# First group of a chunked attention with a maxout product behind it: another order for the first microseconds, with two tiles' scores taken at once

## The chip, the cores and the metric

The kernel runs on one core of one Trainium2 chip. The metric is device time in microseconds (us); a version's time is the median of its runs.

## The reference

```python
# q, k, v: (8, 8, 576, 64) -> batch, heads, sequence, head size; chunks of 64 rows
scores = scale * q_c @ k_c.T            # within each chunk alone, 64 x 64
attn = exp(scores - max) ; attn /= (sum(attn) + 1e-9)
x = (attn @ v_c), heads side by side    # 4608 tokens x 512
h = max(x @ w1, x @ w2, x @ w3)         # 512 -> 768, three products, largest kept
out = h @ w_out                         # 768 -> 512
```

Everything is float32.

## The kernel before

**Tiles and groups.** The 4608 tokens are 36 tiles of 128. Eight of them make two groups of four (columns of a 512 wide moving operand); the other 28 run in four later units. The change touches the first group alone: tiles 0 to 3, with tiles 4 to 7 begun among them, and the loading of all weights, which happens only here.

**Precision.** A float32 product is made of three products of reduced floats: each operand is split into a high part and the rest, and `three` (L186 to L189) multiplies low by high, high by low and high by high. So both the weights (`wh`, `wl`) and the attention's result (`xh`, `xl`) need a high and a low part before a product can start.

**Order.** Nothing is reordered by a scheduler: the engines (PE, DVE, ACT, POOL and the DMA queue SP) take their instructions in the order in which the program calls them, and wait for each other by semaphores. For the first group that order is written by hand in the table `FIRST` (L45), a list of names that `first_group` (L801) calls one after the other. The names are:

- for attention tile *t*: `q`t, `v`t loads; `S`t scores on PE (L237, 16 products of 64x64); `mx`t maximum (DVE, L242); `sub`t subtract it (DVE, L247); `exp`t (ACT, L251); `sum`t (DVE, L195); `eps`t add 1e-9 (DVE, L198); `rec`t reciprocal (DVE, L201); `nrm`t normalise (L204; on POOL with a `p` behind the name, else on DVE); `T`t transposes (PE, L260) into the bank `tp`; `at`t copy of `tp` (ACT, L265); `V`t product with the values (PE, L296); `xh`t and `xl`t high and low part of the result (ACT L303, DVE L307).
- for weight piece *j w* (128 of 768 columns, matrix 1 to 3): `W` load of 512 KB (L154); `A` exponent part (ACT, L163); `B` scaled low words (ACT, L168); `C` shift (DVE, L172); `X` add (POOL with a `p`, else DVE, L176); `H` high part `wh` (ACT, L179); `Y` low part `wl` (POOL with a `p`, else DVE, L182).
- `h`jw with `a` or `b`: products of piece *jw* with columns 0 to 255 (tiles 0 and 1) or 256 to 511 (tiles 2 and 3), 12 matmuls each; with `f` all 512 columns. `F` is the running maximum of the three results, `hh` and `hl` its split.
- `i`n: n idle products of zeros (L795), which only keep PE at work.

The scores of tiles 0 to 3 go into one pair of PSUM banks (`ps_s`), two tiles in turn; `V` writes another pair (`ps_x`), of which tiles 0 and 2 use one half and tiles 1 and 3 the other. The framework follows dependencies by whole PSUM tiles where it can't tell halves apart.

Of the kernel before, what the change touches and what calls it, by code (L numbers as in the profile page):

```python
# [42 lines left out]


FIRST = """  # L45
q0 i13 W01 A01 S0 i5 mx0 q1 sub0 W00 C01 exp0 sum0 S1 mx1 sub1 B01 q2 A00 exp1 W12 eps0 v0 q3 i8 rec0 B00 X01p S2 sum1
H01 mx2 eps1 nrm0p T0 at0 rec1 v1 sub2 nrm1p V0 T1 exp2 C00 S3 X00p xh0 q4 W02 at1 B12 sum2 H00 eps2 V1 rec2 mx3 xh1
nrm2p sub3 T2 S4 xl0 exp3 xl1 sum3 at2 Y00p v2 B02 W10 eps3 rec3 v3 nrm3 A02 W20 h00a V2 A12 C02 W31 T3 Y01p A10 xh2
X02 H02 at3 C10 W11 C12 X12p F00a h01a Y02 V3 xl2 B10 xh3 B31 q5 X10p xl3 A20 W21 A11 h02a F01a H12 F02a B11 C11 W61
W52 Z B20 B21 W40 H10 mx4 sub4 hh0a exp4 W22 C20 X20 W32 Y12 X11 Y10 A31 H11 W30 h01b hl0a h00b C31 h02b A21 H20 X31  # L50
S5 F00b C21 Y11 h12f F01b A40 q6 v4 H31 sum4 W41 B40 X21p h10f F02b H21 Y31 Y20 B30 hh0b eps4 hl0b Y21 C40 mx5 B61
X40p h11f h20f B32 F10f rec4 A22 sub5 W42 A32 C32 S6 A30 X32p h21f B22 W64 F11f F12f W51 C22 B52 H40 hh1f nrm4 hl1f
# [11 lines left out]
def chunk_attn_maxout_kernel(  # L64
# [147 lines left out]
    def bank_of(name):  # L212
        if name not in banks_of:
            banks_of[name] = ps[name].tile([P, 2, 2, 4, 64], F32, name=name[-1])
        return banks_of[name]

    def plain_steps(t, x_of, col):


        st = {}  # L220
# [9 lines left out]

        def scores():
            r = st["r"]
            st["s"] = s = bank_of("ps_s")[:, :, t % 2 if t < 4 or "pair" in st else 0]
            for g in range(4):
                for h, c in quarters:
                    a, b = halves_of[c], halves_of[h]
                    nc.tensor.matmul(out=s[b, c, g, :], lhsT=r[a, 0, 2 * g + h, :], rhs=r[a, 1, 2 * g + h, :],  # L237
                                     start=True, stop=True)
# [70 lines left out]
        def pair(both):  # L309
            st["pair"] = both  # L310

        return dict(q=load_qk, v=load_v, pair=pair, S=scores, mx=maximum, sub=less, exp=exp, sum=total,
                    eps=lambda: st["guard"](), rec=lambda: st["invert"](), nrm=lambda *eng: st["norm"](*eng),
                    T=transpose, at=transposed, bt=blocks, bw=to_scratch, br=from_scratch, V=values, xh=high, xl=low)
# [442 lines left out]
    def hold(name, make):  # L757
        if name not in held:
            held[name] = make()
        return held[name]  # L760
# [90 lines left out]
    def next_load(u, k):  # L851
# [5 lines left out]
        T3=lambda: hold("T3", lambda: late["hold"].tile([P, 2, 3, 256], F32R, name="T3")),  # L857
        s=lambda: hold("s", lambda: late["hold"].tile([P, 5, HALF], F32, name="kept")),
# [163 lines left out]
```

## Time and profile before

| what | value |
|---|---|
| median of 3 runs | 610.44 us (610.24 to 610.49) |
| the profiled execution, its own time | 610.66 us |
| its span on the core | 608.9 us |
| PE busy | 599.4 us (98%) |
| DVE, ACT, POOL busy | 422.8, 289.9, 187.2 us |
| PE on the chain of work that ended last | 92% |

A line of the timeline has the start (us from the span's start), the duration in us, the engine, the source line, the operation, what it writes and reads, and how many; in brackets, where the engine sat idle, for how long and what released it. A line of the windows has the stretch, its length, and the busy time of each engine in it, then the granted clock of PE, the share of the DMA engines and GB/s.

### The profile page before, as it was taken

How to read it: one execution, taken by the hardware profiler on the slowest of the kernel's cores; microseconds unless marked ns; L12 is line 12 of the kernel's file. 1: busy time of each engine (PE TensorE's matmuls, PEld its weight loads, DVE VectorE, ACT ScalarE, POOL GpSimd, SP SyncE). 2: the span in 40 equal slices, each digit the busy share in tenths (PEclk: the TensorE clock that was granted, in tenths of full speed). 3: DMA queues.
4: the chain of work that ended last, by engine and by line, in shares of the span. 5: the costliest groups of instructions: out<-in, count | busy, mean ns of one | idle time of the engine just before them, and what ended most of it. 6: DMA issues, size and time to landing. Idle time of an engine off the chain costs nothing.

```text
span 608.9 us, 12710 instructions
## 1 busy us (share of the span) xinstructions
PE 599.4 (98%) x5045; PEld 520.7 (86%) x5046; DVE 422.8 (69%) x700; ACT 289.9 (48%) x522; POOL 187.2 (31%) x168
## 2 busy tenths in 40 slices
PE   7899999999999999999999999999999999999997
PEld 3788878888899999997888888888888888999997
DVE  4898965768887986894674769936474598244373
ACT  4897734443554554555243344643333355333353
POOL 2522477777232424100250612002424000131300
PEclk9999999999999999999999999999999999999999
DMA  8987667756868998747887894568767444677532
GB/s 336 362 316 269 258 191 266 276 207 238 300 244 300 360 347 289 275 137 252 293 274 242 290 347 162 161 231 285 244 200 262 154 156 123 224 261 259 188 130 79
DMA packets 59484, 148.95 MB, mean 245 GB/s; under 512 B 5665, under 2 KB 24609, under 8 KB 59425
## 3 DMA queue, kind: packets, MB, share of 16 engines
q1 hardware_dynamic: 59424, 148.13, 69.5%
q8 instruction: 40, 0.66, 0.4%
q14 instruction: 20, 0.16, 0.1%
HBM read 116.92 MB, written 31.20 MB: 243 GB/s over the span
## 4 chain that ended last, share of the span: by engine, by line
PE 92%; DVE 5%; ACT 1%; issue 1%; DVEq 0%; ACTq 0%
PE pm L187 28%; PE pm L189 28%; PE pm L188 28%; PE s L237 3%; PE pm L296 3%; PE tp L260 1%; PE pm L795 1%; DVE H L594 1%; DVE stage L519 1%; DVE e L247 0%; DVE sm L195 0%; DVE xl L307 0%; PE s L296 0%; DVE mx L242 0%; DVE X L528 0%
## 5 line engine op out<-in xcount | busy, mean ns | idle before, releaser
L187 PE MATMUL pm<-X,ring 128*128 128x512 f32 (+1 forms) x504 | 184.4, 366 | 0.6 <-ACT kept L626 0.6
L189 PE MATMUL pm<-X,ring 128*128 128x512 f32 (+1 forms) x504 | 182.5, 362 | 0.3 <-issue 0.3
L188 PE MATMUL pm<-X,ring 128*128 128x512 f32 (+1 forms) x504 | 182.4, 362 | 0.0
L626 ACT COPY kept<-pm 128x384 f32<-128x384 f32 (+1 forms) x144 | 76.8, 534 | 155.0 <-PE pm L189 154.9
L187 PEld LDWEIGHTS pm<-X,ring 128*128 128x128 f32 x504 | 94.6, 188 | 11.6 <-ACT kept L626 1.2
L189 PEld LDWEIGHTS pm<-X,ring 128*128 128x128 f32 x504 | 94.6, 188 | 10.4 <-issue 0.6
L188 PEld LDWEIGHTS pm<-X,ring 128*128 128x128 f32 x504 | 94.7, 188 | 9.6
L632 POOL TENSOR_TENSOR kept<-kept 128x384 f32<-128x384 f32 (+1 forms) x24 | 28.6, 1193 | 128.8 <-ACT kept L626 128.8
L629 DVE TENSOR_TENSOR pm<-pm,kept 128x384 f32<-128x384 f32 (+1 forms) x48 | 30.2, 628 | 51.7 <-PE pm L189 51.7
L187 PE MATMUL pm<-xh,wl 128*128 128x512 f32 (+1 forms) x156 | 60.0, 385 | 0.0
L188 PE MATMUL pm<-xl,wh 128*128 128x512 f32 (+1 forms) x156 | 58.4, 374 | 0.3 <-DVE xl L307 0.3
L189 PE MATMUL pm<-xh,wh 128*128 128x512 f32 (+1 forms) x156 | 58.3, 374 | 0.0
L594 DVE TENSOR_TENSOR H<-most,H 128x384 fp32r<-128x384 f32 (+1 forms) x72 | 48.8, 689 | 11.5 <-ACT H L591 11.3
L635 DVE TENSOR_TENSOR most<-pm,most 128x384 f32<-128x384 f32 (+1 forms) x72 | 44.5, 618 | 10.6 <-PE pm L189 9.4
L204 POOL TENSOR_TENSOR e<-e,sm 128x512 f32<-128x512 f32 x27 | 31.5, 1168 | 63.4 <-DVE sm L201 26.5
L632 POOL TENSOR_TENSOR most<-kept 128x384 f32<-128x384 f32 (+1 forms) x12 | 13.8, 1148 | 115.0 <-ACT kept L626 115.0
L242 DVE TENSOR_REDUCE mx<-s 128x8 f32<-128x512 f32 x36 | 24.6, 684 | 33.9 <-PE s L237 33.9
L591 ACT CAST H<-most 128x384 fp32r<-128x384 f32 (+1 forms) x72 | 40.7, 569 | 10.6 <-PE pm L189 9.0
L528 DVE TENSOR_TENSOR X<-stage,X 128x768 fp32r<-128x768 f32 (+1 forms) x28 | 35.0, 1255 | 13.2 <-ACT X L524 13.0
L524 ACT CAST X<-stage 128x768 fp32r<-128x768 f32 (+1 forms) x28 | 26.2, 944 | 29.4 <-DVE stage L519 23.3
L251 ACT ACTIVATE e<-e 128x512 f32<-128x512 f32 x36 | 22.8, 632 | 28.2 <-DVE e L247 28.2
L188 PE MATMUL pm<-H,woh 128*128 128x384 f32 (+1 forms) x96 | 34.8, 363 | 0.1
(119 smaller groups left out, 1060.7 us busy)
## 6 DMA issues: line engine op xcount, KB each, us to landing
ring<-w SPq DMA_DIRECT2D x72, 768.0 KB, 6.1
buf<-in_qk SPq DMA_DIRECT2D x36, 512.0 KB, 5.8
buf<-in_vb SPq DMA_DIRECT2D x36, 256.0 KB, 6.4
ring<-w SPq DMA_DIRECT2D x36, 256.0 KB, 4.1
w<-s SPq DMA_DIRECT2D x9, 768.0 KB, 3.8
out_x<-ao SPq DMA_DIRECT2D x24, 256.0 KB, 2.8
ring<-wo SPq DMA_DIRECT2D x8, 768.0 KB, 4.9
stage<-in_w SPq DMA_DIRECT2D x7, 512.0 KB, 5.1
```

The source lines that it names most:

```text
L187: nc.tensor.matmul(out=o, lhsT=al, rhs=bh, start=first, stop=False, skip_group_check=shared)
L188: nc.tensor.matmul(out=o, lhsT=ah, rhs=bl, start=False, stop=False, skip_group_check=shared)
L189: nc.tensor.matmul(out=o, lhsT=ah, rhs=bh, start=False, stop=last, skip_group_check=shared)
L204: eng.tensor_tensor(out=e, in0=e, in1=sm.unsqueeze(2).broadcast_to([P, 8, 64]), op=ALU.mult)
L524: nc.scalar.copy(out=X[i][:, 0], in_=source[i]())
L528: return lambda: eng.tensor_tensor(out=X[i][:, 1], in0=source[i](), in1=X[i][:, 0].bitcast(F32), op=minus)
L591: nc.scalar.copy(out=H[i, jp][:, 0, :half], in_=hidden_block(i, jp))
L594: nc.vector.tensor_tensor(out=H[i, jp][:, 1, :half], in0=hidden_block(i, jp), in1=H[i, jp][:, 0, :half].bitcast(F32), op=minus)
L626: return lambda: nc.scalar.copy(out=to, in_=o)
L629: return lambda: nc.vector.tensor_tensor(out=o if w else M(jp, q), in0=o, in1=kept(k), op=plus)
L632: nc.gpsimd.tensor_tensor(out=kept(3) if w else M(jp, A22), in0=kept(3), in1=kept(p7), op=plus)
L635: return lambda: nc.vector.tensor_tensor(out=M(jp, q), in0=of, in1=M(jp, q), op=most)
```

## The change

The table gets another order for its first four lines; from `B10 B31 q5` on it is the same. The scores of tiles 0 and 1 follow each other on PE, tile 1's written into the pair of banks that `V` uses later. Eleven idle products stand ahead of them instead of thirteen; the later idle products are 6, 3, 4, 2 and 3 (before: 5 and 8). Piece 01's products come ahead of piece 00's. Tile 0 is normalised on POOL and tile 1 on DVE (before: both on POOL), tile 2 on POOL and tile 3 on DVE as before. `xl0` now comes ahead of `xh1`, and `exp2` behind both.

```diff
-q0 i13 W01 A01 S0 i5 mx0 q1 sub0 W00 C01 exp0 sum0 S1 mx1 sub1 B01 q2 A00 exp1 W12 eps0 v0 q3 i8 rec0 B00 X01p S2 sum1
+q0 i11 W01 A01 B01 q1 C01 X01p W00 S0 S1 mx0 i6 sub0 q2 A00 exp0 mx1 v0 H01 sub1 q3 Y01p S2 i3 exp1 sum0 eps0 rec0 W12
...
-            st["s"] = s = bank_of("ps_s")[:, :, t % 2 if t < 4 or "pair" in st else 0]
+            st["s"] = s = bank_of("ps_x" if t == 1 else "ps_s")[:, :, t % 2 if t < 4 or "pair" in st else 0]
```

On DVE, from the first maximum on, before: `mx_178` is tile 0's maximum, `mx_205` tile 1's, `mx_252` tile 2's; `ao_153` is piece 01's work buffer.

```order
L242 TENSOR_REDUCE mx_178<-s_155 128x2x4
L247 TENSOR_TENSOR e_182<-s_155,mx_178 128x2x4x64
L172 TENSOR_SCALAR ao_153<-ao_153 128x512
L195 TENSOR_REDUCE sm_187<-e_182 128x8
L242 TENSOR_REDUCE mx_205<-s_155 128x2x4
L247 TENSOR_TENSOR e_207<-s_155,mx_205 128x2x4x64
L198 TENSOR_SCALAR sm_187<-sm_187 128x8
L201 RECIPROCAL sm_187<-sm_187 128x8
L195 TENSOR_REDUCE sm_249<-e_207 128x8
L242 TENSOR_REDUCE mx_252<-s_155 128x2x4
```

On DVE at the same place now; tile 0 is `e_202` with `sm_240`, tile 1 `e_214` with `sm_271`, piece 00's buffer `ao_206`.

```order
L242 TENSOR_REDUCE mx_193<-s_159 128x2x4
L247 TENSOR_TENSOR e_202<-s_159,mx_193 128x2x4x64
L242 TENSOR_REDUCE mx_209<-x_176 128x2x4
L247 TENSOR_TENSOR e_214<-x_176,mx_209 128x2x4x64
L195 TENSOR_REDUCE sm_240<-e_202 128x8
L198 TENSOR_SCALAR sm_240<-sm_240 128x8
L201 RECIPROCAL sm_240<-sm_240 128x8
L172 TENSOR_SCALAR ao_206<-ao_206 128x512
L195 TENSOR_REDUCE sm_271<-e_214 128x8
L198 TENSOR_SCALAR sm_271<-sm_271 128x8
L201 RECIPROCAL sm_271<-sm_271 128x8
L204 TENSOR_TENSOR e_214<-e_214,sm_271 128x512
```

Both tiles' subtractions now stand ahead of the first sum, and tile 1's normalising (the last row) has come to DVE.

On POOL, from the first add on, before: `e_182`, `e_207` and `e_266` are tiles 0, 1 and 2, `ao_153` with `wl0_120` piece 01 and `ao_212` piece 00, `ao_416` piece 12.

```order
L176 TENSOR_TENSOR ao_153<-ao_153,xh_128 128x512
L204 TENSOR_TENSOR e_182<-e_182,sm_187 128x512
L204 TENSOR_TENSOR e_207<-e_207,sm_249 128x512
L176 TENSOR_TENSOR ao_212<-ao_212,xh_128 128x512
L204 TENSOR_TENSOR e_266<-e_266,sm_319 128x512
L182 TENSOR_TENSOR wl0_120<-ao_212,wh0_114 128x512
L182 TENSOR_TENSOR wl0_120<-ao_153,wh0_114 128x512
```

On POOL now, in which `e_202` and `e_314` are tiles 0 and 2, `ao_151` is piece 01, `ao_206` piece 00 and `ao_365` piece 02.

```order
L176 TENSOR_TENSOR ao_151<-ao_151,xh_128 128x512
L182 TENSOR_TENSOR wl0_120<-ao_151,wh0_114 128x512
L204 TENSOR_TENSOR e_202<-e_202,sm_240 128x512
L176 TENSOR_TENSOR ao_206<-ao_206,xh_128 128x512
L182 TENSOR_TENSOR wl0_120<-ao_206,wh0_114 128x512
L204 TENSOR_TENSOR e_314<-e_314,sm_348 128x512
L176 TENSOR_TENSOR ao_365<-ao_365,xl_129 128x512
```

The low part of piece 01 has moved ahead of tile 0's normalising, the add and the low part of piece 00 ahead of tile 2's, and piece 02's add has come to POOL behind it.

On ACT, from tile 0's copy out of the transposes' bank on, before; `xs_261` and `xs_316` are `at0` and `at1`, `e_266` and `e_344` are `exp2` and `exp3`, the two rows of L303 `xh0` and `xh1`.

```order
L265 COPY xs_261<-tp_256 128x512 [waits PE_49]
L251 ACTIVATE e_266<-e_266 128x512 [waits DVE_49,Activation_49]
L303 CAST xh_310<-x_269 128x2x4x64 [waits PE_49]
L265 COPY xs_316<-tp_286 128x512 [waits PE_49]
L168 ACTIVATE xl_129<-xl_129 128x512 [waits DMAHW5_49]
L179 CAST wh0_114<-ao_212 128x512 [waits Pool_49]
L303 CAST xh_310<-x_269 128x2x4x64 [waits PE_49]
L251 ACTIVATE e_344<-e_344 128x512 [waits DVE_49,Activation_49]
```

On ACT at the same place now; `xs_282` and `xs_312` are `at0` and `at1`, `e_314` and `e_367` are `exp2` and `exp3`.

```order
L265 COPY xs_282<-tp_273 128x512 [waits PE_49]
L179 CAST wh0_114<-ao_206 128x512 [waits Pool_49]
L265 COPY xs_312<-tp_290 128x512 [waits PE_49]
L303 CAST xh_317<-x_176 128x2x4x64 [waits PE_49]
L303 CAST xh_317<-x_176 128x2x4x64 [waits DVE_49]
L251 ACTIVATE e_314<-e_314 128x512 [waits Activation_49]
L163 ACTIVATE ao_365<-xl_129 128x512 [waits DMAHW1_49]
L251 ACTIVATE e_367<-e_367 128x512 [waits DVE_49,Activation_49]
```

`exp2` has gone from ahead of `xh0` to behind `xh1`, and `xh1` now waits for DVE (for `xl0`), where before it waited for PE alone. On PE the order behind `S3` is now `T0`, `T1`, `V0`, `V1`, three idle products, `h01a`, `T2`, `S4`, `h00a`, `V2`, `T3`, `V3`, `h02a`; before, `T0` to `T2` with `V0`, `V1` and `S4` stood ahead of `h00a`, and behind it `V2`, `T3`, `h01a`, `V3`, `h02a`. From `h01b` on the order is the same.

More of the change, by code (lines that the diff above doesn't have):

```diff
@@ L45 @@
 FIRST = """
-q0 i13 W01 A01 S0 i5 mx0 q1 sub0 W00 C01 exp0 sum0 S1 mx1 sub1 B01 q2 A00 exp1 W12 eps0 v0 q3 i8 rec0 B00 X01p S2 sum1
-H01 mx2 eps1 nrm0p T0 at0 rec1 v1 sub2 nrm1p V0 T1 exp2 C00 S3 X00p xh0 q4 W02 at1 B12 sum2 H00 eps2 V1 rec2 mx3 xh1
-nrm2p sub3 T2 S4 xl0 exp3 xl1 sum3 at2 Y00p v2 B02 W10 eps3 rec3 v3 nrm3 A02 W20 h00a V2 A12 C02 W31 T3 Y01p A10 xh2
-X02 H02 at3 C10 W11 C12 X12p F00a h01a Y02 V3 xl2 B10 xh3 B31 q5 X10p xl3 A20 W21 A11 h02a F01a H12 F02a B11 C11 W61
+q0 i11 W01 A01 B01 q1 C01 X01p W00 S0 S1 mx0 i6 sub0 q2 A00 exp0 mx1 v0 H01 sub1 q3 Y01p S2 i3 exp1 sum0 eps0 rec0 W12
+nrm0p B00 S3 i4 C00 v1 sum1 T0 X00p eps1 rec1 nrm1 at0 i2 W02 mx2 T1 H00 V0 at1 sub2 Y00p xh0 V1 q4 mx3 xl0 i3 xh1 xl1
+exp2 sum2 h01a eps2 rec2 A02 sub3 nrm2p C02 T2 exp3 B02 B12 at2 S4 h00a X02p v2 sum3 eps3 rec3 W10 v3 nrm3 H02 V2 Y02 F00a
+F01a W20 xh2 T3 A12 W31 xl2 at3 A10 C10 W11 C12 X12p V3 xh3 B10 B31 q5 X10p xl3 A20 W21 A11 h02a H12 F02a B11 C11 W61
 W52 Z B20 B21 W40 H10 mx4 sub4 hh0a exp4 W22 C20 X20 W32 Y12 X11 Y10 A31 H11 W30 h01b hl0a h00b C31 h02b A21 H20 X31
```

## The prediction

> **What bounds the kernel now.** I read the windows first: the stretch, its length, PE's busy time in it.
>
> ```profile
> 5.00:10.00 5.00, 4.43 (x75) 2.16 (x75) 2.01 (x4) 1.62 (x3) 0.00 (x0) 1.00 1.02 418
> 10.00:20.00 10.00, 7.17 (x182) 4.88 (x181) 9.34 (x19) 7.72 (x15) 7.32 (x7) 1.00 0.91 336
> 20.00:33.00 13.00, 12.58 (x176) 11.52 (x175) 11.22 (x23) 11.92 (x23) 3.94 (x3) 1.00 1.01 398
> 33.00:100.00 67.00, 67.00 (x496) 54.01 (x498) 52.21 (x85) 43.94 (x79) 33.24 (x28) 1.00 0.70 245
> 100.00:200.00 100.00, 99.71 (x1010) 86.10 (x1001) 80.35 (x120) 45.18 (x79) 52.96 (x49) 1.00 0.75 270
> 200.00:600.00 400.00, 399.38 (x3091) 355.67 (x3089) 265.75 (x451) 177.31 (x324) 88.79 (x76) 1.00 0.68 232
> ```
>
> From 33 to 600 us PE is idle for 0.9 us; all other idling is in front. So whatever the change adds or saves before 33 us arrives at the end one to one, unless those 0.9 us take some of it. The table of waits names PE's longest: the normalised tile, the low part of a result, and one much later.
>
> ```profile
> PE tp L260 <- POOL e L204: 1.9, 2, 1.2
> PE pm L187 <- ACT kept L626: 0.6, 1, 0.6
> PE pm L188 <- DVE xl L307: 0.3, 1, 0.3
> ```
>
> The timeline then gives the front step by step; below I replay the new order with its durations.
>
> ```profile
> 1.19 5.72 PE L795 MATMUL pm<-h 128*128 128x512 bf16 x13 [1.19 <-DVE h L797]
> 5.65 0.67 ACT L163 ACTIVATE ao<-xh 128x512 f32<-128x512 f32 x1 [3.64 <-DMA xh<-in_w]
> 6.83 0.69 PE L237 MATMUL s<-buf 64*64 64x64 f32 x32
> 7.46 1.04 PE L795 MATMUL pm<-h 128*128 128x512 bf16 x4
> 8.32 0.69 DVE L247 TENSOR_TENSOR e<-s,mx 128x512 f32<-128x512 f32 x1
> 8.93 0.42 DVE L172 TENSOR_SCALAR ao<-ao 128x512 uint32<-128x512 uint32 x1
> 11.83 0.20 DVE L201 RECIPROCAL sm<-sm 128x8 f32<-128x8 f32 x1
> 12.11 1.04 POOL L204 TENSOR_TENSOR e<-e,sm 128x512 f32<-128x512 f32 x1 [0.49 <-DVE sm L201]
> 12.41 0.69 DVE L195 TENSOR_REDUCE sm<-e 128x8 f32<-128x512 f32 x1 [0.38 <-ACT e L251]
> 12.84 0.60 ACT L179 CAST wh<-ao 128x512 fp32r<-128x512 f32 x1
> 14.16 1.04 POOL L204 TENSOR_TENSOR e<-e,sm 128x512 f32<-128x512 f32 x1 [1.00 <-DVE sm L201]
> 14.77 0.63 ACT L251 ACTIVATE e<-e 128x512 f32<-128x512 f32 x1 [0.28 <-DVE e L247]
> 15.31 0.58 ACT L303 CAST xh<-x 128x512 fp32r<-128x512 f32 x1
> 17.34 1.04 POOL L204 TENSOR_TENSOR e<-e,sm 128x512 f32<-128x512 f32 x1 [0.44 <-PE x L296]
> 18.34 2.54 POOL L182 TENSOR_TENSOR wl<-ao,wh 128x512 fp32r<-128x512 f32 x2
> 18.44 0.66 PE L260 MATMUL tp<-ident,e 128*128 128x128 f32 x4 [1.16 <-POOL e L204]
> 18.44 1.28 DVE L307 TENSOR_TENSOR xl<-x,xh 128x512 fp32r<-128x512 f32 x2
> 19.68 0.39 PE L187 MATMUL pm<-xh,wl 128*128 128x256 f32 x1
> 19.90 0.28 PE L188 MATMUL pm<-xl,wh 128*128 128x256 f32 x1
> 21.18 0.69 DVE L204 TENSOR_TENSOR e<-e,sm 128x512 f32<-128x512 f32 x1
> 22.02 0.63 PE L260 MATMUL tp<-ident,e 128*128 128x128 f32 x4
> 24.13 0.71 PE L296 MATMUL x<-xs,buf 64*64 64x64 f32 x32
> 26.29 0.35 PE L187 MATMUL pm<-xh,wl 128*128 128x256 f32 x1
> 26.98 0.39 PE L188 MATMUL pm<-xl,wh 128*128 128x256 f32 x1 [0.34 <-DVE xl L307]
> 30.75 0.68 DVE L182 TENSOR_TENSOR wl<-ao,wh 128x512 fp32r<-128x512 f32 x1
> 31.37 0.69 PE L237 MATMUL s<-buf 64*64 64x64 f32 x32
> ```
>
> The four tiles pass one after the other: `exp2` at 14.77, `nrm2` on POOL 17.34, `T2` 18.44, first real product 19.68, `nrm3` on DVE 21.18, `T3` 22.02, `V3` 24.13, and the second matmul of `h01b` at 26.98, the last wait. From there PE is full; `S5` stands at 31.37.
>
> One more thing decides much here: some DVE instructions stand still while POOL works.
>
> ```profile
> 15.62 1.29 POOL L176 TENSOR_TENSOR ao<-ao,xh 128x512 int32<-128x512 int32 x1 [0.42 <-ACT e L251]
> 16.16 0.78 DVE L198 TENSOR_SCALAR sm<-sm 128x8 f32<-128x8 f32 x1
> 120.29 2.54 POOL L407 TENSOR_TENSOR f<-wh,wl 128x512 f32<-128x512 f32 x2
> 121.91 1.47 DVE L204 TENSOR_TENSOR e<-e,sm 128x512 f32<-128x512 f32 x1
> ```
>
> The tiny add L198 ends at 16.94, just behind POOL's 16.91, and the normalising L204, 0.69 alone, ends 0.55 behind POOL's 122.83. So `eps` and a `nrm` on DVE do not run beside a POOL instruction; they wait for its end. Subtractions and sums (8.32, 12.41) keep 0.69 beside POOL.
>
> **The change, step by step** (names as in the table, times us).
>
> *Idle products and clock.* Eleven at the first ones' spacing (5.72/13, say 0.43) end at 5.9 instead of 6.8, so `S0` may start 0.9 earlier. The idle products came 0.43 apart before 6.8 and 0.26 or less from 7.46 on, so PE's real clock doubled about 6.8; the column of granted clock doesn't show it. `S0` may thus run at half speed, 0.63 or 1.26 long. [...] By either the sum stays the same, since the next step does not wait for `S0`. Cost 0: `exp0` stands behind `A00` on ACT, and `A00` waits for the fourth load. The second landed at 5.65; two loads of 512 KB at 418 GB/s take 1.25 each, so 8.15. `A00` to 8.85 (0.67), `exp0` to 9.4 (instructions on ACT overlap by 0.1). Before, `exp0` started at 9.05: 0.3 won.
>
> *That gain is lost on POOL.* `H01` 9.3 to 9.9 (0.60), `Y01` on POOL 10.0 to 11.25 (2.54/2). `eps0` would be due at 10.1 to 10.5 but waits until 11.27; `rec0` 11.5; `C00` 11.4 to 11.85 holds POOL back a little; `nrm0` 11.8 to 12.8. `X00` follows at once on POOL, 12.8 to 14.1 (1.29). `nrm1`, now on DVE, is ready at 13.1, waits for 14.1 and ends 0.55 later, 14.65. On POOL before, `nrm1` ended at 15.2 (14.16 and 1.04). "Side by side" therefore gives 0.5, not 1.
>
> *One serial chain to the first product.* `T1` 14.7; `V0` stands behind it, 15.1 to 15.8. Tiles 0 and 1 share the bank, and the new order alternates engines on it: `xh0` 15.85 to 16.45 (0.58), `V1` 16.5 to 17.2 (0.71), `xl0` 17.25 to 17.95 (0.69), `xh1` 18.0 to 18.6, `xl1` to 19.3. The first matmul can start at 18.6, the second waits for `xl1`: 19.35. Before it started at 19.90; 0.55 won.
>
> *Tile 2 is late.* `mx2` and `sub2` follow `nrm1` on DVE, 14.55 to 16.0, but `exp2` is queued on ACT behind `xh1`: 18.5 to 19.1, where it ran at 14.77. `sum2` to 19.9, `eps2`, `rec2` 20.35, `nrm2` on POOL 20.45 to 21.5 (before 17.34), `T2` 21.5 (before 18.44). `h01a` ends at 20.85, so PE waits 0.65, a new wait. `S4`, then `h00a` 22.5 to 24.
>
> *Tile 3 is later still.* `sub3` stands behind `rec2`, 20.25 to 20.95; `exp3` to 21.65, `sum3` to 22.35. `eps3` meets `X02`, on POOL 22.3 to 23.6 now, and waits for its end; `rec3` 23.8, `nrm3` 23.9 to 24.55 (before 21.18). `T3` 24.6 (before 22.02). `at3` on ACT stands behind `xh2` and `A12`: 25.8 to 26.4, so `V3` starts at 26.45 instead of 24.13: 2.3 late. PE waits 1.2 for it.
>
> *What is given back.* Before, `h02a` didn't cover `xh3` and `xl3`: the second matmul of `h01b` waited until 26.98. Now `xh3` ends 27.8 and `xl3` 28.5, beside `h02a` (27.1 to 28.5); `h01b` begins at 28.5 without waiting, its second matmul at 28.65, 1.65 late. The same adding up of durations for the old order puts `S5` at 31.0 against the trace's 31.37, since it counts no time for PE's switches between kinds of matmul; the new order has a few more of them, so I take 1.75.
>
> *One more wait.* The low part of the first weight piece of `h12f` was written at 30.75, 0.6 ahead of `S5`. ACT and DVE have more left to do behind `xh3` now, which puts that row at 33.0, until 33.7, and `h12f` 0.3 behind `S5`'s end. Bounds: 0, if they catch up, to 0.6, the row's own length; I take 0.25.
>
> *Loads.* SP issues `v2` only when `V0` is done, 15.8 instead of 15.2, so `W10` and those behind it come up to 0.7 later; PE comes 2 later. Cost 0, cover 1.3. The other idle products end ahead of the transposes they precede: 0.
>
> *Sum:* 1.75 + 0.25 = +2.0. The profiled execution took 610.66, so 612.7; it stands 0.22 over the median 610.44, so 612.4. A difference within 0.2% (1.2 us) can't be told from no change by a measurement of this kernel.
>
> **Rivals.**
> 1. *Not slower: the delay is absorbed.* If the two later waits (0.6 for ACT's `kept`, and the 0.3 left of the 0.9) are fixed in time and not tied to PE, a late PE finds them over: +2.0 - 0.85 = +1.15, 611.6, within 0.2%. It decides as soon as the front's delay is under 2.05. Against it: ACT's `kept` is a copy of what PE made, so it moves with PE. Chance 0.10.
> 2. *DVE and POOL do run side by side.* Then `eps0` isn't held, `nrm1` ends at 13.0 to 13.8 and `eps3` at 22.5; the serial chain and `exp2`'s place stay. Worth 0.6: +1.4, 611.8, still slower. Against it: the two pairs of rows above. Chance 0.08.
> 3. *The clock falls back.* With gaps of 0.65 to 1.2 ahead of `T2` and `V3`, PE could drop to half speed. `h01a`, 1.4 long, would take 2.8, of which 0.65 was waiting: +0.75, 613.2. [...] Against it: before, gaps of 1.16 ahead of `T2` left the next products at full spacing. Chance 0.10.
> 4. *No later tile:* if tiles 2 and 3 kept their distance to the first product, all would come 0.55 earlier, 609.9, no change that can be told. It decides whether `exp2` runs before 16.5, which its place in ACT's row excludes. Chance 0.05. For a gain over 0.2% I see no mechanism; 0.03 is for what I don't see.
>
> **How the numbers follow.** The forecast +2.0, with its own spread of 0.5, has 0.64; with rivals 2 and 3 slower has 0.82; rivals 1 and 4 make same 0.15; faster 0.03. The range 611.2 to 613.4 leaves out rival 4 and the outer parts of 1 and 3, under 2 in 10.
>
> **What the changed profile would show.** `exp0` near 8.8, `nrm1` on DVE about 1.5 long, second real matmul near 19.4, `exp2` near 18.5, PE waiting for POOL ahead of `T2` and for ACT ahead of `V3` (1.2), `S5` near 33.1, PE full from there. I am wrong if `exp2` stands near 16, if `nrm1` takes 0.7 with POOL at work, or if `S5` is under 32.5 with the end not moved.

## The result, and the profile after

The changed kernel is slower: 613.9 us median of 6 runs (612.94 to 615.04) against 610.63 (610.24 to 610.96) in the same session, a ratio of 1.006, 95% interval 1.005 to 1.007. That is 3.3 us, where 2.0 was forecast; the direction was right, and the time lies 0.5 above the range. Its profiled execution took 613.28, a span of 611.5 after 608.9: 2.6 more. So two things are to be explained: 2.6 instead of 2.0 in the profile, and another 0.7 between the profile and the median.

The stretches of time first, as in the prediction (start and end, length, PE, PEld, DVE, ACT, POOL, granted clock, share of DMA, GB/s):

```profile
5.00:10.00 5.00, 3.33 (x100) 2.08 (x102) 3.57 (x6) 3.02 (x6) 1.30 (x2) 1.00 1.03 412
10.00:20.00 10.00, 6.88 (x137) 4.25 (x131) 8.13 (x14) 4.95 (x9) 4.90 (x4) 1.00 0.84 311
20.00:33.00 13.00, 11.17 (x170) 10.23 (x169) 10.34 (x20) 10.61 (x20) 4.94 (x4) 1.00 0.99 375
33.00:100.00 67.00, 66.71 (x504) 54.06 (x504) 53.95 (x90) 44.63 (x82) 32.24 (x28) 1.00 0.70 238
...
200.00:600.00 400.00, 399.35 (x3092) 355.71 (x3091) 265.71 (x451) 177.88 (x326) 89.70 (x76) 1.00 0.68 234
```

Between 20 and 33 us PE is now busy for 11.17 where it was 12.58. Behind that it is full as before, so what the front loses arrives at the end. The table of PE's waits names the places behind 20 us:

```profile
PE x L296 <- ACT xs L265: 1.2, 1, 1.2
...
PE tp L260 <- POOL e L204: 0.7, 1, 0.7
...
PE pm L188 <- issue: 0.4, 1, 0.4
...
PE pm L187 <- DVE wl L182: 0.3, 1, 0.3
```

The first is `V3` waiting for `at3`, the second `T2` waiting for `nrm2`, the last the new bubble ahead of `h12f`: the three that the prediction named, at 1.2, 0.65 and 0.25. The third is something else, of which more below. The timeline, the rows that answer to those quoted of before:

```profile
1.19 4.15 PE L795 MATMUL pm<-h 128*128 128x512 bf16 x11 [1.19 <-DVE h L797]
8.78 0.62 ACT L251 ACTIVATE e<-e 128x512 f32<-128x512 f32 x1
10.15 1.14 DVE L198 TENSOR_SCALAR sm<-sm 128x8 f32<-128x8 f32 x1
13.02 1.50 DVE L204 TENSOR_TENSOR e<-e,sm 128x512 f32<-128x512 f32 x1
18.18 0.58 ACT L303 CAST xh<-x 128x512 fp32r<-128x512 f32 x1 [1.61 <-DVE xl L307]
18.66 0.63 ACT L251 ACTIVATE e<-e 128x512 f32<-128x512 f32 x1
19.55 0.39 PE L188 MATMUL pm<-xl,wh 128*128 128x256 f32 x1 [0.34 <-DVE xl L307]
20.70 1.04 POOL L204 TENSOR_TENSOR e<-e,sm 128x512 f32<-128x512 f32 x1 [4.54 <-DVE sm L201]
21.80 0.66 PE L260 MATMUL tp<-ident,e 128*128 128x128 f32 x4 [0.67 <-POOL e L204]
22.65 1.16 DVE L198 TENSOR_SCALAR sm<-sm 128x8 f32<-128x8 f32 x1
27.07 0.69 PE L296 MATMUL x<-xs,buf 64*64 64x64 f32 x32 [1.16 <-ACT xs L265]
33.64 0.69 PE L237 MATMUL s<-buf 64*64 64x64 f32 x32
```

Line by line: `exp0` at 8.78 (forecast 8.75 to 8.85); `eps0` stretched to 1.14 and `eps3` to 1.16 by POOL; `nrm1` on DVE 1.50 long; `xh1` waiting 1.61 for `xl0`; `exp2` at 18.66 (18.5); the second real product at 19.55 (19.35); `nrm2`, `T2`, `V3` at 20.70, 21.80 and 27.07 (20.45, 21.5, 26.45). `S5` comes at 33.64, forecast 33.1, before 31.37.

### The profile page after: what moved, and what is told of

It reads as the page before. It is cut to its first block, busy times and chain, and to the rows that moved or that the text cites. A ratio compares the mean times of both kernels' runs of the same rounds, so it can differ in the third digit from the quotient of the medians.

```text
span 611.5 us, 12710 instructions
## 1 busy us (share of the span) xinstructions
PE 598.7 (98%) x5046; PEld 520.8 (85%) x5049; DVE 424.5 (69%) x700; ACT 289.8 (47%) x522; POOL 187.6 (31%) x168
## 4 chain that ended last, share of the span: by engine, by line
PE 87%; DVE 5%; ACT 1%; issue 1%; ACTq 0%; DVEq 0%
PE pm L187 27%; PE pm L188 27%; PE pm L189 27%; PE pm L296 2%; PE s L237 2%; PE tp L260 1%; DVE H L594 1%; DVE stage L519 1%; PE s L296 0%; DVE X L528 0%; ACT H L591 0%; DVE ao L716 0%; DVE xs L270 0%; DVE mx L242 0%; DVE e L204 0%
## 5 line engine op out<-in xcount | busy, mean ns | idle before, releaser
L187 PEld LDWEIGHTS pm<-xh,wl 128*128 128x128 f32 x156 | 29.4, 188 | 6.9 <-ACT xh L303 1.2
```

Of the source, the lines that this page charges most:

```text
L187: nc.tensor.matmul(out=o, lhsT=al, rhs=bh, start=first, stop=False, skip_group_check=shared)
```

## The experiments

Four theories were tested; the expectations name them. A: the new order of the front's steps (`exp2` late, tiles 2 and 3 behind it) costs the same in every run. B: in quiet stretches PE's clock falls to half for a while. C: PE has to wait for its own instructions. D: the front of the kernel before follows the moment at which the clock rises, that of the changed kernel doesn't.

**The changed kernel again** (no edit).

> The changed kernel once more, for its spread and a second profile. Theory A (the late exp2 and late tiles 2 and 3 set the delay; the rest is the same in every run): a profile with first real product near 18.8, T2 near 21.8, V3 near 27.1, S5 near 33.6, and a median near 613.4, 1.0045 to 1.005 of before. Theory B (on top of A, PE is so little used between 16 and 20 us, 2.1 of 4, that its real clock falls back in some runs): again a median near 613.9 with runs 2 us apart, and a profile of a slower run shows a stretch behind 18.8 in which the products come 0.24 apart instead of 0.12.

613.85 us median of 6 runs (613.47 to 614.99), 1.006 of before (1.0045 to 1.0074). The profile is A's, 0.2 late throughout: `T2` 22.00, `V3` 27.27, `S5` 33.85. The median is not A's 613.4 but the 613.9 that B expected, and so the first profile was one of the quicker runs. But B's fall shows in one run alone: one of the six had a mean granted clock of 0.997, the others 0.999 or 1.000.

**`exp2` earlier** (ACT: between `xh0` and `xh1`).

```diff
-xh0 V1 q4 mx3 xl0 i3 xh1 xl1
-exp2 sum2 h01a eps2
+xh0 exp2 V1 q4 mx3 xl0 i3 xh1 sum2 xl1
+h01a eps2
```

> The changed kernel with the exponential of tile 2 between xh0 and xh1 on ACT, and its sum between xl0 and xl1 on DVE. Theory A: exp2 at 16.4 instead of 18.7, but its sum still waits for xl0; adding up durations puts T2, V3 and S5 0.7 earlier, so 0.7 us off the changed kernel's time, about 613.2 if that is 613.9. Rival (the chain xh0, V1, xl0, xh1, xl1 on the shared bank is what counts): no gain, the first product stays at 18.8 and S5 at 33.6. Theory B: the first product doesn't move, the quiet stretch stays, so the runs stay 2 us apart.

The timeline of this kernel: `exp2`, `nrm2`, `T2`, `S5`.

```profile
16.74 0.63 ACT L251 ACTIVATE e<-e 128x512 f32<-128x512 f32 x1
20.25 1.04 POOL L204 TENSOR_TENSOR e<-e,sm 128x512 f32<-128x512 f32 x1 [3.85 <-DVE sm L201]
21.35 0.66 PE L260 MATMUL tp<-ident,e 128*128 128x128 f32 x4
33.20 0.69 PE L237 MATMUL s<-buf 64*64 64x64 f32 x32
```

Against the second profile of the changed kernel, whose `exp0` stands nearly where this one's does (8.99 and 9.07), `nrm2`, `T2` and `S5` are 0.65 earlier, although the first product isn't (19.09 and 19.02). So `exp2`'s place delays tiles 2 and 3 apart from the chain to the first product, by 0.65 of the 3.4 that `T2` is late; its sum still waits behind `xl0` here. The span was 610.8, 0.7 under the changed kernel's 611.5. The median hardly moved, 613.71 (612.57 to 615.73): two of the six runs had a mean clock of 0.997.

**Tile 2 early as a whole.**

```diff
-V0 at1 sub2 Y00p xh0 V1 q4 mx3 xl0 i3 xh1 xl1
-exp2 sum2 h01a eps2 rec2 A02 sub3 nrm2p C02 T2 exp3
+V0 at1 V1 sub2 exp2 Y00p q4 mx3 xh0 sum2 eps2 rec2 nrm2p xh1 xl0 xl1
+sub3 h01a A02 exp3 C02 T2
```

> The changed kernel with V1 ahead of xh0, both high parts ahead of both low parts, exp2 ahead of xh0, and its sum, reciprocal and normalising in the gap ahead of xl0; sub3 and exp3 follow at once. Theory A: first product 17.9, second 19.2, T2 20.6 without a wait, V3 25.5, S5 1.0 earlier than in the changed kernel; time lower by 1.0, about 612.9 if that is 613.9. Theory B: the quiet stretch ahead of T2 is gone as well, so the spread shrinks to that of the kernel before (0.7) and the median falls further, to 612.3. If neither place matters: 613.9.

It was slower, 614.33 us (611.52 to 615.66), not faster, and this profile shows why. Windows of 3.41 us in it, counted from the moment at which its clock rose (start and end, length, PE busy, granted clock, DMA):

```profile
12.54:15.95 3.41, 3.17 (x63) 1.00 0.90 359
15.95:19.37 3.42, 1.43 (x58) 1.00 0.61 206
19.37:22.78 3.41, 3.21 (x15) 0.50 0.98 366
22.78:26.19 3.41, 3.41 (x81) 1.00 1.00 393
```

The clock fell to half at 19.37 and rose again at 22.78, 3.41 us later: behind a window in which PE was busy for 1.43 of 3.42. Five of the six runs had a mean clock of 0.994 to 0.997, which one or two such windows make (half of 3.41 in 612 is 0.003). The one without ran in 611.52. So B's fall is seen here, and a mean clock of 0.997 is taken as its sign in runs without a profile. The three idle products that this edit had dropped, 0.65 us, would by adding up have made PE busy for 0.61 of the window instead of 0.42.

**The gaps filled** with idle products, in the changed kernel's order.

```diff
-xl0 i3 xh1
+xl0 i7 xh1
-C02 T2 exp3
+C02 i2 T2 exp3
-X12p V3 xh3
+X12p i5 V3 xh3
```

> The changed kernel with fourteen idle products in place of three in PE's waits: seven instead of three ahead of the first real product, two ahead of T2, five ahead of V3. Nothing else moves. Theory A: they lie inside waits, S5 moves by under 0.1, time and spread as in the changed kernel. Theory B: PE is busy through the quiet stretch, the clock doesn't fall back, so the spread falls under 1 us and the median to the fastest runs of the changed kernel, 613.0.

617.38 us (615.03 to 617.76): 3.5 slower than the changed kernel, which neither theory had. Up to 187 us the profile equals the changed kernel's within 0.1 (`S5` 33.59). Then PE stands still, and waits for nothing that the profile shows:

```profile
PE s L237 <- issue: 1.7, 1, 1.7
```

The changed kernel has a row of that kind, 0.4, ending at 191.55. The trace has 40 pieces of 16 KB on `q8`, marked as instructions (packets, MB, share of the DMA engines):

```profile
q8 instruction: 40, 0.66, 0.4%
```

By the trace's packet records one of them starts at 189.19 here, while PE runs a burst of 128 small products that began at 187.62. PE stands still from 189.70, four products short of the burst's end, and goes on at 191.41. In all fourteen waits of this kind in the profiles PE goes on 2.2 to 2.5 us behind the start of a piece, and wherever the wait stands near 190 us PE had started 3728 to 3733 instructions, weight loads included. Fourteen idle products in place of three put that point eleven products earlier in the program, into the burst. This is theory C. Why a piece starts when it does, no trace shows; that the burst empties a queue of PE's is the author's guess. Three of the five runs also had a mean clock of 0.997; no profile caught where. But a stretch of 3.41 us, slid along the profiled run from 8 us on, has PE busy for 0.61 of it or more everywhere except at this wait:

```profile
188.01:191.42 3.41, 1.70 (x117) 1.00 0.68 196
```

That is 0.50, about as little as in the windows behind which the clock fell elsewhere (1.66 and 1.69 us, below). So the wait itself is the likely place of the falls in this kernel. A window at half clock would cost 1.7 where PE is full, by the author's estimate (half of 3.41), and the three runs with 0.997 are 2.1 longer than the two without. It isn't shown, since in the profiled run the clock stayed up.

**Eleven more idle products in the kernel before**, inside its waits.

```diff
-S0 i5 mx0
+S0 i7 mx0
-nrm0p T0 at0
+nrm0p i3 T0 at0
-nrm1p V0 T1
+nrm1p i2 V0 T1
-sub3 T2 S4
+sub3 i4 T2 S4
```

> The kernel before with eleven more idle products inside PE's waits of the front: seven instead of five ahead of S1, three ahead of T0, two ahead of V0, four ahead of T2. Theory C (some 3730 PE instructions from the start, PE waits for its own instructions, which come in pieces of 16 KB; the load starts when a burst of 128 small products has emptied the queue at 186.7 us, so each product added ahead takes away 0.17 us of the work that covers the load): the front doesn't move (S5 31.4), the wait behind 187 us grows from 0.3 to 1.7 or more, and the time from 610.4 to 612 or more, with runs in which the clock falls for one window (mean granted clock 0.997) up to 614. Theory A (only the order of the front's steps counts): 610.4 as before.

612.58 us (610.74 to 614.77), 1.0041 of before (1.0027 to 1.0054): 2.3 slower, with `S5` at 31.47. The wait:

```profile
PE s L237 <- issue: 1.6, 1, 1.6
```

C holds, in a kernel whose order wasn't touched: idle products that cost nothing where they stand cost 1.6 at 187 us, and four of nine runs had a mean clock under 0.998. Here too the stretch of 3.41 us with the least of PE lies at the wait (0.52, from 185.46); in the front none has under 0.88. Between 24 and 29 idle products in all, though, the wait was 0.3, 0, 0.8 and 0 (four profiles of the kernel before, 26) and 0.4, 0 and 0.4 (three of the changed one, 29): there chance rules, and C doesn't explain the difference of the two kernels.

**Three fewer in the changed kernel** (`i6` to `i3` behind `S1`).

> The changed kernel with three instead of six idle products behind S1, so that it has as many idle products as the kernel before. Theory C: the front doesn't move (S5 33.6 to 33.8), the wait for instructions near 191 us is up to 0.5 shorter, the median falls from 613.85 by 0.2 to 0.5. Theory A: 613.85. Rival (the clock): PE is less busy between 7 and 10 us, 0.4 to 0.5 of a window, and falls back in some runs: mean clock 0.997 there and 1 us more, since little of the work there is PE's.

614.39 us (612.87 to 615.29). The profiled run, with `S5` at 33.66 and no wait for instructions, was the quickest; the other four had a mean clock of 0.996 or 0.997. So the rival took place in them, as far as the mean tells: a stretch of 3.41 us from 8.4 us on has PE busy for 0.46 of it. In the profiled run the windows began at 7.11 and 10.52 and had 0.67 and more; no profile caught the fall. What C expected can't be told from this run.

**Tile 2 early, with the quiet stretch filled** and idle products taken out elsewhere.

```diff
-S3 i4 C00
+S3 i1 C00
-at0 i2 W02
+at0 i0 W02
-xh1 xl0 xl1
+xh1 i5 xl0 xl1
```

> tile2_early with five idle products between V1 and the first real product, and five fewer where PE is busy anyway (three ahead of T0, two ahead of T1), so the count is that of the kernel before. Theory B in the form that tile2_early's profile gave (a window of 3.41 us in which PE is busy 0.42 lets the clock fall to half for the next one, 0.54 does not): no window under 0.54 is left here, so the mean clock is 0.999 or more in every run, first product near 18.2, T2 near 21.0, S5 0.8 to 1.0 ahead of the changed kernel's 33.6, median 612.9 or less with the changed kernel at 613.85. If the quiet stretch is not the cause: 614.3 as tile2_early, with 0.997 in most runs.

612.14 us (611.48 to 613.47), 1.0033 of before (1.0021 to 1.0044), 2.2 under tile2_early. Its timeline: `nrm2`, `T2`, `T3`, `S5`.

```profile
18.08 1.04 POOL L204 TENSOR_TENSOR e<-e,sm 128x512 f32<-128x512 f32 x1 [2.03 <-DVE sm L201]
20.66 0.60 PE L260 MATMUL tp<-ident,e 128*128 128x128 f32 x4
24.07 0.66 PE L260 MATMUL tp<-ident,e 128*128 128x128 f32 x4
32.45 0.69 PE L237 MATMUL s<-buf 64*64 64x64 f32 x32
```

`T2` no longer waits, and `S5` is 1.2 ahead of the changed kernel's 33.64. A and B hold together: half of the loss goes with this order once the clock is kept up. Not all of it is tile 2's place, since the second real product comes 0.3 earlier too (19.26 for 19.55). `V3` still waits 1.2 for `at3`, as in the changed kernel; no run moved that. Not as expected: three of the six runs still had 0.997. Taking products out ahead of `T0` and `T1` had left a stretch from 11.1 us on with 0.47; in the profiled run no window began there.

**Eleven idle products in the kernel before**, that part of the change alone (`i13` to `i11`).

> One part of the change alone: the kernel before with eleven instead of thirteen idle products in front. By the order of steps S0 starts at 6.0 instead of 6.8, sub0, exp0 and all of tiles 0 to 3 come up to 0.4 earlier if the data of the second load don't hold them: 610.0 at best, 610.4 if they do. Theory C adds: two products fewer ahead, so the wait for instructions shrinks from 0.3 to 0, another 0.2 at most. Rival: with two products fewer the clock rises a window later in more runs, S0 and S1 run at half speed, 610.4 to 611.

609.97 us (608.62 to 611.37), 0.9993 of before (0.9983 to 1.0003): a gain of 0.35 that can't be told from none. But the profile has `S5` at 30.21, 1.16 ahead of the profile of before, where the author had put two products at 0.4 at most. Here it rose at 5.30, there at 6.76. That led to D, by which the first products of the kernel before wait for nothing but PE (in the profile of before `S0` follows the idle products at 6.83 without a wait for data). C's expectation failed: the wait for instructions was 0.5, not 0.

**Three more profiles of the kernel before** (no edit).

> The kernel before once more, for a second profile. [...] With the rise at u under 6.8, S0 comes (6.8 - u) / 2 earlier than 6.83, and tiles 0 to 3 and S5 with it, S5 down to 30.0 from 31.4; the changed kernel's S5 stays at 33.6 to 33.85 for rises at 4.17, 4.46 and 7.1. Rival (the front doesn't follow the clock): S5 31.4 whatever the rise.

> The kernel before, a third profile. Theory D: T3 at 22.0 for a rise of the clock at 6.8 or later, 20.7 for one at 4.1, in between (u - 4.1) / 2 more. Rival: T3 doesn't follow the rise.

> The kernel before, a fourth profile, with the same expectations: T3 from 20.7 to 22.0 with the moment of the rise by theory D, apart from it by the rival.

**And one of the changed kernel.**

> The changed kernel, a third profile. Theory D: its front waits for the fourth load and for POOL, not for PE, so T3 at 25.3 to 25.5 and S5 at 33.6 to 33.9 wherever the clock rises. Rival: a late rise moves T3 by up to 1.3 here too.

The rise is where the trace's clock records begin; it shows in the row of the idle products too. Of the first of these kernels, the thirteen products and `T3`:

```profile
1.19 4.39 PE L795 MATMUL pm<-h 128*128 128x512 bf16 x13 [1.19 <-DVE h L797]
20.71 0.63 PE L260 MATMUL tp<-ident,e 128*128 128x128 f32 x4
```

Of the third:

```profile
1.19 4.91 PE L795 MATMUL pm<-h 128*128 128x512 bf16 x13 [1.19 <-DVE h L797]
21.23 0.63 PE L260 MATMUL tp<-ident,e 128*128 128x128 f32 x4
```

All seven profiles together:

| kernel | clock rises | `T3` | `S5` | instruction wait near 190 | time |
|---|---|---|---|---|---|
| before | 6.76 | 22.02 | 31.37 | 0.3 | 610.66 |
| before_again | 4.09 | 20.71 | 30.95 | 0 | 610.51 |
| before_again2 | 4.59 | 20.94 | 30.37 | 0.8 | 610.11 |
| before_again3 | 5.14 | 21.23 | 31.75 | 0 | 610.65 |
| changed | 4.46 | 25.26 | 33.64 | 0.4 | 613.28 |
| again | 4.17 | 25.46 | 33.85 | 0 | 613.57 |
| again2 | 6.60 | 26.60 | 34.98 | 0.4 | 614.74 |

`T3` of the kernel before follows the rise at half its rate, as D says: 4.09 to 6.76 is 2.67, and `T3` moves 1.31. The changed kernel's doesn't follow it: 4.17 and 4.46 stand in the wrong order, and the other kernels with its front had `T3` at 25.20 and 25.28 with rises at 7.10 and 7.11. But `S5` of the kernel before keeps only part of the gain, not all of it as D had it. In two of the four PE waits for instructions a first time, inside `V3` (row of before_again's waits):

```profile
PE x L296 <- issue: 0.7, 1, 0.7
```

It was 0.9 in before_again3 and nothing in the other two. The mean of `S5` is 31.1, so the profile on which the prediction stood was late by 0.3 only.

again2 is one of the longer runs of the changed kernel. Its `T3` and `S5` are not those that D expected (25.3 to 25.5, 33.6 to 33.9), and its profile shows two causes. The third and fourth load landed at 7.54 and 8.89 instead of 6.89 and 8.19, and `exp0` came at 9.48, 0.7 late. This front hangs on its loads one to one: in changed, again, filled and after_3fewer the fourth load landed between 8.10 and 8.39, and `S5` came 25.43 to 25.49 behind it in each. And the clock fell:

```profile
13.43:16.84 3.41, 2.37 (x43) 1.00 0.62 249
16.84:20.25 3.41, 1.69 (x36) 1.00 0.73 237
20.25:23.67 3.42, 3.42 (x15) 0.50 0.97 353
23.67:27.08 3.41, 3.41 (x81) 1.00 1.03 420
```

From the second product to `S5` it took 14.75 instead of 14.09 and 14.10: the fall cost 0.65 here. The window ahead of it, with the wait for the shared bank and the late first product in it, was busy for 1.69 of 3.41. Laid where PE has least to do behind 8 us, a stretch of 3.41 us has 0.49 in the profile of changed, 0.54 in again, and 0.53 in each of the four profiles of the kernel before. That fits a clock that falls in the changed kernel now and then, when a window happens to lie there, and not in the other.

**Eight idle products in the kernel before** (`i13` to `i8`), so that `S0` doesn't wait for them.

> The kernel before with eight instead of thirteen idle products in front, so that S0 starts when its data are there (4.4 us) and not behind the idle products. Theory D: S0 at 4.7 whatever the clock does, exp0 near 7.4 to 8.0, S5 29.8 to 30.3; five products fewer ahead also shorten the wait for instructions near 187 us. Median 609.2, a ratio of 0.998. Rival 1: exp0 then meets the second and third loads (6.93, 8.17), tiles 1 to 3 don't follow, 610.0 as with eleven. [...]

611.0 us (608.52 to 612.88), no difference that can be told (0.9993 to 1.0022). `S0` came at 4.71 and `exp0` at 7.36 as expected, `S5` and the median did not (`S5` at 33.15 for 29.8 to 30.3). PE stood still inside `V1`, from 15.6 to 17.4, and the clock fell behind that window, for two windows:

```profile
13.88:17.29 3.41, 1.66 (x67) 1.00 0.99 379
17.29:20.70 3.41, 3.28 (x41) 0.50 0.57 196
20.70:24.12 3.42, 3.42 (x44) 0.50 0.99 341
24.12:27.53 3.41, 3.41 (x56) 1.00 1.02 410
```

The three runs with a mean clock of 0.999 or 1.000 took 608.52, 608.83 and 608.96, the others up to 612.88. **With the products spread instead of dropped** (26 in all, seven of them new ones ahead of `T0`, `V0`, `T2`):

> before_8ramp with its idle products spread: eight in front, four and seven instead of five and eight further on, and seven new ones in the waits ahead of T0, V0 and T2 (26 in all, as in the kernel before). Theory D with B: S0 at 4.7 whatever the clock does, and no window after the rise in which PE is busy under 0.55, so the clock doesn't fall and the runs come out as the undisturbed ones of before_8ramp (mean clock 1.000: 608.5 to 609.0): median 608.9, a ratio of 0.9975. Rival (the wait for instructions at the end of V1, 1.8 in before_8ramp, comes from the faster front and not from chance): S5 no earlier than 31.4, median 610.5 or more.

609.21 us median (607.99 to 612.75), ratio 0.9997 (0.998 to 1.0014): three runs of eleven with a fallen clock were left, and the wait in `V1` was there again, so it comes with the faster front, as the rival says:

```profile
PE x L296 <- issue: 1.8, 1, 1.8
```

`S5` came at 31.14, no earlier than the kernel before on average, if ahead of the rival's 31.4. No version tried is faster than the kernel before by more than its interval.

**Two parts undone in the changed kernel.** First the normalising side by side (`nrm1` to `nrm1p`):

> The changed kernel with nrm1 back on POOL (behind X00), the side-by-side part undone alone. By the prediction's step (nrm1 on DVE waits for X00's end and ends 0.5 ahead of one on POOL): nrm1 starts at 14.1 and takes 1.04, T1 at 15.2, and everything behind it up to S5 is 0.5 later, S5 34.1 to 34.2, time 0.5 over the changed kernel's profiled 613.3 to 613.6. Rival (both sides run at once, so DVE gains 1.0): S5 34.6.

`nrm1` on POOL starts at 13.88, `T1` at 14.98 after 14.67, `S5` at 33.98: 0.3 later, and 0.4 when counted from the fourth load's landing, where 0.5 was expected; the time, 614.33, has a wait for instructions of 0.7 in it. Then the second bank (`"ps_x" if t == 1 else "ps_s"` back to `"ps_s"`):

> The changed kernel with the scores of tile 1 in the other half of tile 0's bank again, in the changed order (S0, S1, then mx0). Then mx0 waits for S1, which waits for the third load (6.9): mx0 7.7 instead of 6.7, exp0 9.2 instead of 8.8, nrm0 12.0, nrm1 13.5 and S5 0.4 later, 34.1; time 0.4 over the changed kernel's. If the banks don't matter, because POOL's X01, Y01 and X00 hold the front anyway: S5 33.6 to 33.85.

`exp0` 9.31, `nrm1` 13.55, `S5` 34.17: 0.5 later than in the changed kernel's first profile, 0.3 than in its second, and 0.4 counted from the fourth load, as expected. So both parts do win what they are for, by one profile each. They are small beside the order of tiles 2 and 3 that comes with them.

## Why the prediction was right, and where not

*The bound* (what is lost ahead of 33 us arrives at the end): right. From `S5` to the end it is 577.5 in the profile of before and 577.8 in that of after, and the bubble is in that.

*POOL holds DVE, and "side by side" gives 0.5:* right in kind, `nrm1` took 1.50 beside POOL; undone, it cost 0.3 to 0.4. Rival 2 is out: `nrm1` ended at 14.52, 0.54 behind POOL's `X00` (12.69 to 13.98). Two readings were loose, though nothing hangs on them. The subtraction quoted at 8.32 had no POOL instruction beside it (the first comes at 10.33); the one at 11.03 had, and took 0.69 too. And the table of waits leaves out two of 0.7, PE for DVE's subtractions and for ACT's copy, ahead of the first product.

*One chain to the first product:* 19.55 for 19.35; `V0` slipped by 0.13 and the rest along the chain.

*Tiles 2 and 3 late because `exp2` stands behind `xh1`:* right as far as it was undone: exp2_mid and tile2_filled get 0.65 and 1.2 of `S5`'s delay back. That the rest lies in `V3`'s wait for `at3` is read from the profiles alone.

*1.75 for the front, 0.25 for the bubble:* this is the first step that failed, too small by 0.5 and 0.1. `S5` moved by 2.27, and the step from `S5` to the next product grew from 0.63 to 0.99. The 1.75 sets durations added up for the new order (28.65 for the second matmul of `h01b`) against the trace of the old one (26.98). Yet by the prediction's own words the same adding up came out 0.37 early for the old order, 31.0 for 31.37; 0.1 was put on for it. Like with like, the front is 1.65 + 0.37, or 2.0, and the bubble's 0.36 makes it 2.4, where the profile moved by 2.6. The new chain slipped along its length: `V0` by 0.13, `T2` by 0.3, `V3` by 0.6, the first product of `h01b` by 0.7 (29.23 for 28.5). One piece can be named: `T2` to `h00a` was put at 1.0 and took 1.21, and the old order's rows, 18.44 and 19.68, already had 1.24.

*"It stands 0.22 over the median, so 612.4":* this is the second step that failed. It took a shift that is the same in every run, and a median of three runs. Over six runs the kernel before has 610.63, only 0.03 under its profile, so 0.2 of the 0.22 was chance. And the changed kernel's profile, 613.28, was one of its quicker runs, 0.6 under its median. With the 0.5 and 0.1 above, these make up the 1.5 between 612.4 and 613.9.

What lies behind the 0.6 is known in part. The changed kernel's front follows its fourth load, which landed between 8.10 and 8.89 in the profiles of this front, and it lost 0.65 in the one fall profiled. But only two of its thirteen runs had a mean clock of 0.997, and none of the six behind the 613.9 (63 runs of the kernel before had none under 0.999). So those runs had late loads, waits for instructions or something else; no profile shows which. The kernel before spreads for another reason: its front gains from an early clock, and over four profiles its `S5` is 0.3 earlier than in the first. With the means of `S5`, 31.1 and 34.2, and 0.36 for the bubble the sum is 3.4, against 3.3 between the medians; since one of the three profiles of the changed kernel is among its longest runs, that agreement may be luck.

*Rival 3, the clock falls back,* had a chance of 0.10 with +0.75 on top; it took place in two runs of thirteen, cost 0.65 in the one profiled, and came not through the gaps ahead of `T2` and `V3` that the prediction named, but behind the half-busy stretch ahead of the first product. The row offered against it, a gap of 1.16 that had left the clock alone, was no argument: the stretch of 3.41 us with the least of PE in that profile still has 0.53, and the three falls profiled came behind windows with 0.42 to 0.50 (1.43 to 1.69 us). *Rivals 1 and 4* didn't happen: the 0.6 behind ACT's `kept` is there as before, and tiles 2 and 3 fell back.

*Loads at no cost:* right for those that SP issues late; no wait of PE's behind 20 us names a load in the profile of after. The fourth load was rightly named as what `exp0` waits for (8.19 for 8.15), but it and the third weren't thought of as varying.

Open are four things: what made the changed kernel's unprofiled runs longer than its profile; why the first piece of instructions began at 15.0 in before_8ramp and before_8fill, where the other kernels have it between 12.8 and 14.2; why the clock stayed low in before_8ramp through a window with PE busy for 3.28 of 3.41; and where the clock fell in the runs of filled, before_11more and after_3fewer that no profile caught.

## What to carry to other kernels

When a step is moved forward, look at what its engine now does ahead of the step that it has overtaken: here one exponential was queued behind two conversions, two later tiles came some 3 us late, and improvements of about 0.4 each were lost in it. Moving it up won 0.65 to 1.2 back. A profile is one draw: before a shift is added to a median, ask which steps of each version hang on something that differs from run to run (the clock's rise, a load), and take a second profile. And when two orders are compared by adding up durations, add up both: what the sum leaves out on one side it must leave out on the other. Idle products aren't free because they stand in a wait: fourteen in place of three moved the place of PE's wait for instructions, and it grew from 0.4 to 1.7.

## What the runs showed of the hardware

- The clock rose at 4.09 us in before_again, at 6.76 in before and at 7.11 in after_3fewer, with the first idle product at 1.19 in each. The three falls profiled lasted 3.41 us (tile2_early, again2) or twice that (before_8ramp), and two of them began four times 3.41 us behind the rise of their own run: 5.71 to 19.37 in tile2_early, 6.60 to 20.25 in again2. In tile2_early the products behind the fall came 0.21 apart, in the profile of the changed kernel 0.12.
- The falls came behind windows in which PE was busy for 1.43 (tile2_early), 1.66 (before_8ramp) and 1.69 (again2) of 3.41. The clock stayed up behind 1.64 in before_8fill, around a stretch with 1.70 in filled, and behind 1.97 in before_8ramp. PE's longest single wait in the three windows ahead of the falls was 1.19, 1.83 and 0.75 us.
- In the fourteen waits of PE behind which the profiles show no other engine (`issue`) it went on 2.2 to 2.5 us behind the start of one of the 16 KB pieces. Ten of them were 0.3 to 0.9 long, two 1.6 and 1.7 where they fell into a burst of small products (before_11more, filled), and two 1.8, inside `V1`, when the front was made faster (before_8ramp, before_8fill).
- In the profile of the changed kernel the normalising on DVE took 1.50 beside POOL (13.02) for 0.69 alone (24.08), and the add over 128x8 1.14 and 1.16 for 0.17; in that of before a subtraction beside POOL (11.03) kept 0.69.
